# A hand-written instruction order of a convolution, norm and SwiGLU kernel is replaced: products, output steps, hidden sums and DMAs in new places

## The chip, the cores and the metric

The kernel runs on one core of one Trainium2 chip. The metric is the device time of one execution in microseconds (us); the median of the runs shown is given. The core has TensorE (PE; its weight loads, PEld, overlap its matmuls), VectorE (DVE), ScalarE (ACT), GpSimd (POOL) and SyncE (SP), which here issues nearly all DMAs. Each engine works through its own instructions in the order in which they were emitted.

## The reference

32,768 tokens of 192 values in fp32 (8 batches of 4,096 positions). First a causal convolution over the last 7 positions, its taps a softmax for each of 8 heads; then a SwiGLU feed-forward with 1,536 hidden units:

```python
w = np.exp(w - w.max(-1)); w = w / (w.sum(-1) + 1e-09)
out = np.einsum('hk,bskhg->bshg', w, x_unf)          # x_unf: 7 shifted views
...
rms = np.sqrt(np.mean(x * x, axis=-1, keepdims=True) + 1e-06)
xn = x / rms * rms_g
g = xn @ w_gate
silu = g * (1.0 / (1.0 + np.exp(-g)))
val = xn @ w_val
return (silu * val @ w_out).astype(np.float32)
```

## The kernel before

**Tiling.** The tokens go in 32 pairs of two 512-token halves (1,024 tokens). Pair 0 is computed plainly (lines 1099, 1117), pair 1 with plain gate/value products (line 890), pairs 2 to 31 in a block scheme of Strassen's kind: gate and value matrices and the two halves form 2x2 blocks, and sums of blocks are multiplied instead of blocks. Every period of the loop (w = 1 to 32) works on one pair.

**Products and steps.** A period's TensorE work is listed in `LINE`: 68 products, each with a group j = 0 to 5 (words such as P5.0, Ad.3, Q3.5), then 42 output steps (o1 to o7, each with j). A product (line 918) is six matmuls: three parts of the split operand by two halves, which write the two banks of a *bank pair*. An output step (line 945) is six smaller matmuls that multiply hidden values by blocks of the output weights. A product may open a *cell* (j and a letter a to d): P1, P5 and the A words open one. Four bank pairs exist for all cells and for the output's accumulators (`open`, `give`); a cell holds its pair until its silu and its multiply are done.

**Words of the order.** `ORDER` lists everything that is issued in one period, for all engines, in the order of emission. `pN` is the next N words of `LINE`; a minus sign behind a word means the previous pair, a plus sign the next one, two plus signs the one after. Otherwise the first letter is the engine (V VectorE, A ScalarE, G GpSimd, S SyncE) and the rest is the act:

- ga.j to gd.j: silu of a cell's gate half (line 995); ma.j to md.j: multiply with its value half (line 1002), after which the cell's pair is free.
- f1.j, f3.j: copies of finished cells (line 683; f1 opens cell b with a copy of a); f4.j, f5.j: sums that open c and d (line 989).
- h1.j to h4.j: sums of hidden values for the output steps (line 972), on VectorE or GpSimd.
- x1 to x4: sums of token blocks (line 840). n, l, d with a group 0 to 4: the three steps that split the next pair's tokens into parts (cast at line 683, differences at 826 and 828).
- cv0 to cv6: the convolution's taps (line 453; the first, on ScalarE, at 449); sq, red, pow, bc, mul: the norm (lines 464 to 503).
- pl.h: put of a normed head into DRAM (line 1062); ft.i: fetch of it, transposed, as token blocks (line 654); ld.h: load of a head of x (line 154); st: store of outputs (line 1051). The last four are DMAs in SyncE's queue.
- c1, c2, s7, C22, C21, T11 to T22: copies, sums and transposes that finish the output (lines 683, 1019, 960).

**Ring.** The split weights lie prepared in DRAM; ten slots of 192 KB hold those in use. When the last product with a slot has been issued, the next load into that slot is issued in SyncE's queue (line 798), behind whatever stands there. A load starts when its slot's last product is done, and 48 of them come in a period.

**Other orders.** `FIRST` is the order of w = 1, with W for a step of the weight preparation (lines 762 to 775) and R for the start of the ring. `PLAIN` begins the list of pair 1. The lead-in before the loop (pair 0: `conv_first`, conversion of the weights at lines 299 to 346, `START`, `LATER`) is written out by hand too. `hold` (line 226) makes a copy that the first weight loads wait for, so that x is loaded first.

Of the kernel before, what the change touches and what calls it, by code (L numbers as in the profile page):

```python
# [20 lines left out]
def kernel(  # L21
# [10 lines left out]
    nc = tc.nc  # L32
# [3 lines left out]
    H, K = weight.shape  # L36
# [21 lines left out]
    PAIRS = B * NB  # L58
# [17 lines left out]
        "a0 b0 c0 d0 o1.0 a1 b1 c1 d1 o1.1 a2 b2 c2 d2 o1.2 a3 b3 c3 d3 o1.3 a4 b4 c4 d4 o1.4",  # L76
        "a5 b5 c5 d5",
    )
    ORDER = (
# [14 lines left out]
    )  # L94
    FIRST = (
# [14 lines left out]
    )  # L110
    LINE = (
# [7 lines left out]
    )  # L119
# [10 lines left out]
    x_sb = {}  # L130
# [31 lines left out]
    def load_part(p, h, eng):  # L162

        if h == 0:
            x_sb[p] = xs.tile([P, TB + HALO, GS], F32, name="xh")
        load_head(p, p // NB, (p % NB) * PT, h, eng)
# [57 lines left out]
    def hold(t):  # L224

        nc.scalar.copy(out=t, in_=x0[:, -t.shape[1] :, 0])

# [158 lines left out]
    scr = {}  # L386

    ys = {}

    def conv_first(mine, share, give):  # L390

        t = x_sb.pop(0)
# [3 lines left out]
        for i, k in enumerate([theirs[0], mine[-1]] + theirs[1:]):  # L396
# [4 lines left out]
            if k == theirs[-1]:  # L401
                cuts = (0, H // 2, H - give)
            for lo, hi in zip(cuts, cuts[1:]):
# [4 lines left out]
                for c in range(4):  # L408
# [4 lines left out]
                    )  # L413
        for k in mine:
            xk = t[:, k : k + NJ, :]
            for h in range(share if k == mine[-1] else 0, H):
                hs = slice(h * GS, (h + 1) * GS)
                w = taps[:, h, k : k + 1]
                if k == mine[0]:
                    nc.vector.tensor_scalar(  # L420
                        out=y[:, :, hs], in0=xk[:, :, hs], scalar1=w, scalar2=None, op0=ALU.mult
                    )
                else:
                    nc.vector.scalar_tensor_tensor(
                        out=y[:, :, hs], in0=xk[:, :, hs], scalar=w, in1=y[:, :, hs],
                        op0=ALU.mult, op1=ALU.add,
                    )
# [416 lines left out]
    class Pair:  # L844
        def __init__(self, p):
            self.p = p
            self.bk, self.o_sb, self.sg = {}, {}, {}
            self.open_half, self.turned = {}, [0, 0]
            self.line = self.products()

# [75 lines left out]
        def step(self, form, k):  # L926
            b = ACC[form]
            if form in (1, 7) and b not in self.bk:
                full4.discard(self.open(b, False))
            fresh = form in (1, 7) and k == 0  # L930
            src = hs[:, k, :] if form == 5 else self.hv(k, LEFT[form])
# [126 lines left out]
    def put_away(p, h, eng):  # L1058
        if h == 0:
            scr[p] = dram.tile([D, PT], F32, name="xd")  # L1060
# [101 lines left out]
    def done(it):  # L1162
# [13 lines left out]
    LATER = (  # L1176
        (30, "s"), (35, "v"), (45, "v"), (47, "O"), (50, "O"), (53, "O"), (55, "n"), (60, "t"),
    )
# [11 lines left out]
    nc.vector.tensor_reduce(out=tp[:], in_=own[:], axis=AX.X, op=ALU.add)  # L1190
    load_in(0, nc.sync)
    load_out(0)
    load_out(1)
    load_in(1, nc.sync)
    conv_first((1, 3, 5, 6), 0, 2)
    nc.gpsimd.memset(zeros, 0.0)
# [78 lines left out]
    run([w for row in FIRST for w in row.split()], 1)  # L1275
    for w in range(2, PAIRS + 1):
        run([w for row in ORDER for w in row.split()], w)
# [28 lines left out]
```

## Time and profile before

| | us |
|---|---|
| median of 3 runs (2469.66, 2471.25, 2470.25) | 2470.25 |
| the profiled execution | 2473.39 |
| its span, first to last instruction | 2471.6 |
| start of w = 2, 3, 32 on TensorE | 214.0, 288.8, 2461.7 |
| TensorE's last matmul | 2465.9 |

The profiled execution is 3.1 us longer than the median. A period is counted from the first matmul of one pair's list to that of the next. TensorE's granted clock is 1.00 in every window. The 2,173 us from w = 3 to w = 32 are 29 periods of the same order; the 289 us before them hold pair 0, the weight preparation and pair 1. Mean lengths of one instruction, from the table of groups, in us:

| line, engine, what | us |
|---|---|
| 995 ACT silu | 0.60 |
| 1002 DVE multiply | 0.69 |
| 989 DVE f4, f5 | 1.23 |
| 972 DVE hidden sum; on POOL | 0.72 to 0.75; 1.29 to 1.73 |
| 826 DVE difference; on POOL | 1.22; 2.40 |
| 828 DVE difference | 1.25 to 1.38 |
| 840 x sum on DVE; on POOL | 0.69 to 1.25; 1.28 to 1.30 |
| 453 DVE tap | 1.81 |

### The profile page before, as it was taken

To read this page: it belongs to the slowest core of one execution; us is meant where nothing else is said; L and a number is where in the kernel's file an instruction comes from. 1 tells how busy PE (TensorE), PEld (TensorE's weight loads), DVE (VectorE), ACT (ScalarE), POOL (GpSimd) and SP (SyncE) were. 2 spreads that over 40 slices of the span, in tenths; PEclk is the share of its full clock that TensorE was granted. 3 is DMA by queue.
4 is the path that set the end of the run, shared out by engine and by line. 5 is a ranking of instruction groups with operands and counts; after the bars stand their busy time and mean duration, and the time that the engine had idled before them with its cause. 6 is when DMAs were issued, how large, how long until landed. Compare 5 with 4: busy or idle time off the path is not lost.

```text
span 2471.6 us, 69198 instructions
## 1 busy us (share of the span) xinstructions
PE 2452.5 (99%) x29136; PEld 1894.3 (77%) x29136; DVE 2024.1 (82%) x2530; ACT 1016.2 (41%) x1431; POOL 833.3 (34%) x624
## 2 busy tenths in 40 slices
PE   8999999999999999999999999999999999999999
PEld 5547778887777777877777778777787787777777
DVE  8688888889888789888888787888888888888864
ACT  6443434433344434344334344333444343443332
POOL 0541343423343323334333434233433333333322
PEclk9999999999999999999999999999999999999999
DMA  7364678666677666786667776666776666876653
GB/s 152 60 207 125 175 184 211 179 171 170 164 200 195 181 165 172 176 207 181 190 158 178 179 202 186 176 168 168 199 197 187 165 172 169 203 192 188 159 161 95
DMA packets 716392, 430.55 MB, mean 174 GB/s; under 512 B 510330, under 2 KB 702386, under 8 KB 716082
## 3 DMA queue, kind: packets, MB, share of 16 engines
q1 hardware_dynamic: 712336, 425.21, 66.5%
q8 instruction: 230, 3.77, 0.7%
q10 hardware_dynamic: 3746, 0.92, 0.2%
q14 instruction: 80, 0.66, 0.1%
HBM read 366.96 MB, written 58.98 MB: 172 GB/s over the span
## 4 chain that ended last, share of the span: by engine, by line
PE 90%; DVE 3%; DMA 3%; SPq 1%; issue 1%; POOL 1%; ACT 1%; DVEq 0%; POOLq 0%; ACTq 0%
PE ps L918 55%; PE ps L945 35%; DMA xb<-xd 1%; DMA ht<-in_moe_w_val_dram 1%; DMA ring<-wd 1%; SPq L154 0%; DVE ht L972 0%; POOL part L775 0%; SPq L238 0%; DVE ht L1117 0%; DVE ht L1002 0%; DVE part L771 0%; DVE y L453 0%; DMA x<-in_x_dram 0%; DVE ps L989 0%
## 5 line engine op out<-in xcount | busy, mean ns | idle before, releaser
L918 PE MATMUL ps<-part,ring 64*128 64x512 f32 x12240 | 1422.0, 389 | 2.6 <-DMA ring<-wd 1.9
L918 PEld LDWEIGHTS ps<-part,ring 64*128 64x128 f32 x12240 | 1152.9, 184 | 257.8 <-DVE ps L989 12.5
L995 ACT ACTIVATE tt<-ps 128x512 f32<-128x512 f32 x744 | 438.9, 599 | 715.8 <-PE ps L918 661.7
L1002 DVE TENSOR_TENSOR ht<-ps,tt 128x512 f32<-128x512 f32 x744 | 498.0, 686 | 254.3 <-ACT tt L995 252.2
L945 PE MATMUL ps<-ht,wo_sb 128*32 128x384 f32 (+2 forms) x7272 | 468.3, 380 | 0.8 <-POOL wo_sb L337 0.8
L972 POOL TENSOR_TENSOR ht<-ht 128x512 f32<-128x512 f32 x180 | 272.2, 1520 | 543.9 <-PE ps L945 536.4
L945 PE MATMUL ps<-ht,x 128*32 128x256 f32 (+2 forms) x6696 | 439.1, 379 | 1.3 <-DVE ht L972 1.3
L945 PEld LDWEIGHTS ps<-ht,wo_sb 128*32 128x32 f32 x7272 | 325.1, 110 | 114.5 <-issue 14.5
L945 PEld LDWEIGHTS ps<-ht,x 128*32 128x32 f32 x6696 | 299.6, 110 | 90.9 <-DVE ht L972 1.6
L989 DVE TENSOR_TENSOR ps<-ps,tt 128x1024 f32<-128x1024 f32 x240 | 295.8, 1233 | 54.3 <-ACT tt L683 22.8
L453 DVE SCALAR_TENSOR_TENSOR y<-xh,tp,y 128x1536 f32<-128x1536 f32 x186 | 336.6, 1810 | 0.2
L683 ACT COPY ps<-ps 128x1024 f32<-128x1024 f32 (+1 forms) x151 | 134.6, 891 | 408.0 <-PE ps L918 336.5
L972 POOL TENSOR_TENSOR hs<-ht 128x512 f32<-128x512 f32 x120 | 155.0, 1292 | 262.6 <-DVE ht L1002 262.6
L683 ACT COPY tt<-ps 128x384 f32<-128x384 f32 (+1 forms) x182 | 151.7, 833 | 218.6 <-PE ps L945 154.9
L482 POOL TENSOR_SCALAR r<-r 128x8 f32<-128x8 f32 x31 | 6.1, 197 | 504.5 <-DVE r L477 504.4
L945 PE MATMUL ps<-hs,x 128*32 128x128 f32 (+2 forms) x2232 | 161.4, 379 | 0.0
L972 DVE TENSOR_TENSOR ht<-ht 128x512 f32<-128x512 f32 x192 | 135.0, 717 | 15.2 <-PE ps L945 12.6
L945 PEld LDWEIGHTS ps<-hs,x 128*32 128x32 f32 x2232 | 106.9, 110 | 29.6
L828 DVE SCALAR_TENSOR_TENSOR part<-part,xb 128x1024 fp32r<-128x1024 f32 x87 | 120.1, 1381 | 0.0
L972 DVE TENSOR_TENSOR ht<-hs,ht 128x512 f32<-128x512 f32 x156 | 109.2, 747 | 11.3 <-PE ps L945 10.7
L826 POOL TENSOR_TENSOR part<-xb,part 128x1024 fp32r<-128x1024 f32 x29 | 69.7, 2403 | 124.0 <-PE ps L918 82.1
L503 POOL TENSOR_TENSOR xh<-y,s 128x1536 f32<-128x1536 f32 x30 | 89.9, 2995 | 15.1 <-DVE s L495 8.6
(133 smaller groups left out, 1417.6 us busy)
## 6 DMA issues: line engine op xcount, KB each, us to landing
ring<-wd SPq DMA_DIRECT2D x1440, 192.0 KB
xb<-xd SPq DMA_DIRECT2D x60, 512.0 KB
xd<-xh SPq DMA_DIRECT2D x240, 96.0 KB
xh<-in_x_dram SPq DMA_DIRECT2D x192, 105.0 KB
xb<-xd SPq DMA_DIRECT2D x60, 256.0 KB
out_dram<-o_sb SPq DMA_DIRECT2D x126, 96.0 KB
out_dram<-o_sb SPq DMA_DIRECT2D x62, 128.0 KB
wd<-part SPq DMA_DIRECT2D x5, 1152.0 KB
```

The costliest lines, as they stand in the source:

```text
L453: nc.vector.scalar_tensor_tensor(out=y, in0=xk, scalar=w, in1=y, op0=ALU.mult, op1=ALU.add)
L482: nc.gpsimd.tensor_scalar(out=r, in0=r, scalar1=s / D, scalar2=s * 1e-6, op0=ALU.mult, op1=ALU.add)
L503: e.tensor_tensor(out=yn[p].rearrange("p a t -> p t a"), in0=y, in1=ss[:].rearrange("p (t o) -> p t o", o=1).to_broadcast([P, TB, GS]), op ...
L683: nc.scalar.copy(out=dst, in_=src)
L826: e.tensor_tensor(out=split_of(g, 1).bitcast(F32R), in0=src, in1=high, op=ALU.subtract)
L828: nc.vector.scalar_tensor_tensor(out=split_of(g, 2).bitcast(F32R), in0=high, scalar=1.0 + SPLIT, in1=src, op0=ALU.mult, op1=ALU.subtract,)
L918: nc.tensor.matmul(out=self.both(j, c)[:, h, :], lhsT=left[HALF[h]], rhs=right[HALF[h]], start=(first and q == 0), stop=True, skip_group_c ...
L945: nc.tensor.matmul(out=self.acc(b)[i * Q : (i + 1) * Q, at : at + n], lhsT=left, rhs=cols, start=fresh, stop=True, skip_group_check=True, ...
L972: engine[eng].tensor_tensor(out=dst, in0=a, in1=b, op=op)
L989: nc.vector.tensor_tensor(out=self.both(j, c), in0=self.both(j, "b"), in1=s5, op=ALU.add)
L995: nc.scalar.activation(out=tt[:, t, :], in_=self.both(j, c)[:, 0, :], func=AF.Silu)
L1002: nc.vector.tensor_tensor(out=self.hv(j, "abcd".index(c)), in0=self.both(j, c)[:, 1, :], in1=tt[:, t, :], op=ALU.mult,)
```

## The change

Products, output steps and all other words of a period stand in a new order (`LINE`, `ORDER`); w = 2 has an order of its own, `SECOND`, which has the same words with stores, loads and the previous pair's end in other places. Pair 1 keeps the old sequence of output steps, now written out in `PLAIN`. Per period, two net hidden sums, x4 and l.0 go from GpSimd to VectorE; cv1 and cv2 go from the end of the period before into the period itself, among the products; d.4 goes from the beginning of a period to the end of the one before. In SyncE's queue the fetches, loads and stores stand in other places: puts and fetches in the last third of the products, loads and stores mostly among the output steps. Words that issued nothing (ft.1, ft.3) are left out. Since words can now stand in any order, three helpers no longer ask for "the first index" but for "not there yet" (`load_part`, `put_away`, `step`). In `FIRST`, ma.1 stands right behind ga.1, ahead of four steps of the weight preparation, and the loads of the pair after and the first tap (cv0) stand earlier. In the lead-in the copy of `hold` goes from ScalarE to VectorE and behind VectorE's first tap (and so do the issues of the first weight loads), one instruction of the first convolution goes from VectorE to ScalarE, and in `LATER` the conversions of the output weights (O) stand earlier.

```diff
@@ -74,48 +74,68 @@
     )
     PLAIN = (
         "a0 b0 c0 d0 o1.0 a1 b1 c1 d1 o1.1 a2 b2 c2 d2 o1.2 a3 b3 c3 d3 o1.3 a4 b4 c4 d4 o1.4",
-        "a5 b5 c5 d5",
+        "a5 b5 c5 d5 o7.0 o7.4 o1.5 o7.3 o7.1 o7.2 o2.5 o2.0 o7.5 o6.1 o6.5 o6.0 o6.4 o6.2",
+        "o6.3 o2.3 o4.0 o4.3 o5.2 o5.3 o5.1 o4.5 o5.0 o4.4 o2.2 o4.1 o2.1 o5.4 o4.2 o5.5 o2.4",
+        "o3.3 o3.1 o3.0 o3.5 o3.2 o3.4",
     )
     ORDER = (
-        "p2 Vl.2 VC22- VT11- p3- Vd.4 VT22- VT21- Vcv3+ p3- Af1.0 Af3.0 VT12- p4 Aga.0 Vcv4+",
-        "Vf4.0 Vma.0 p2 Vcv5+ p1 Sst0.4- Sst0.2- Sst1.4- Agb.1 p5 Agc.0 Aga.1 Vmb.1 Vf5.0 p3",
-        "Vcv6+ Vma.1 Vmc.0 Agb.0 Agd.0 p2 Vmb.0 Asq+ Vmd.0 p3 Af1.2 Agc.3 Af3.2 p2 Vred+ p1",
-        "Vmc.3 p1 Vf4.2 Aga.2 Vma.2 p1 Gpow+ Vbc+ p1 Vf5.2 Gmul+ p3 Spl.0+ Agd.3 Vmd.3 p3",
-        "Spl.1+ Spl.2+ Agd.2 Agb.2 Agc.2 Vmd.2 Vmb.2 Vmc.2 Spl.3+ p6 Spl.4+ Agc.1 p1 Af1.4",
-        "Spl.5+ Spl.6+ Spl.7+ Vmc.1 p3 Agd.1 Vmd.1 p2 Af3.4 p1 Vf4.4 p4 Aga.4 Sft.0+ Sft.1+",
-        "Vma.4 Vf5.4 Agb.3 p3 Agd.4 Agc.4 Vmb.3 Vmd.4 Vmc.4 p2 Sft.2+ Sft.3+ Sst0.3- Sld.0++",
-        "Sft.4+ Sft.5+ Agb.4 Sld.1++ Sld.2++ Sst1.1- Gh1.2 Vmb.4 Gh1.1 Gh3.1 Gh1.0 p1 Sld.3++",
-        "Sst0.0- Gh3.2 Sld.4++ Sst0.1- Sld.5++ Af1.5 Sld.6++ Gh1.3 Sld.7++ p1 Af3.5 p2",
-        "Sst1.0- Sst1.2- Sst1.3- Vh1.4 Vh3.4 Vh3.0 Vf4.5 An.0+ Aga.3 p3 Vma.3 p2 Gl.0+ Gh3.3",
-        "Gx3+ Vf5.5 Aga.5 Agc.5 Vma.5 Vmc.5 p3 Vx1+ Agd.5 Agb.5 An.1+ Vx2+ p11 Vmd.5 Vh2.4",
-        "Vmb.5 Vd.0+ Vh1.5 Vh3.5 Vh2.3 Vh2.1 Vh2.5 Gx4+ Gh2.0 An.4+ Ac1 p5 Vh2.2 p1 An.3+ p4",
-        "An.2+ As7 p1 Ac2 Acv0++ Vh4.0 Vd.3+ Vd.2+ p11 Vh4.5 Vl.3+ Vh4.3 Vl.4+ Vcv1++ Vl.1+",
-        "Vcv2++ Vd.1+ p3 Gh4.1 VC21 Gh4.4 Gh4.2",
+        "p1- VT11- p1- p2 Af1.0 VT21- VC22- p4- Vcv2+ p1- VT22- p1- Vl.2 p1 Vcv3+ Af3.0 VT12-",
+        "p1 Vf4.0 p2 Aga.0 p1 Vcv5+ Vma.0 p3 Vf5.0 Agc.0 p1 Agb.1 p1 Vmc.0 Vcv6+ p4 Agb.0",
+        "Vmb.1 Vcv4+ p4 Agd.0 Agc.3 Vmb.0 Vcv1+ Aga.1 p2 Vmd.0 Vma.1 Asq+ p1 Af1.2 p1 Vmc.3",
+        "Agd.3 p1 Vred+ p3 Af3.2 Aga.2 Vmd.3 Gh1.0 Vf4.2 Gh3.0 Vma.2 Gpow+ p5 Agc.2 p1 Vf5.2",
+        "Sst1.1- p2 Vbc+ Agc.1 Vmc.2 p1 Vmc.1 Agd.2 Gmul+ Agb.2 Vmd.2 p4 Af1.4 Sst0.3- Vmb.2",
+        "Agd.1 p1 Spl.5+ Spl.2+ p1 Gh1.2 p1 Spl.4+ Vmd.1 p1 Af3.4 p1 Gh1.1 Aga.4 Spl.0+ p1",
+        "Vf4.4 p1 Spl.7+ Spl.1+ Vma.4 p3 Vf5.4 Agb.3 Vh3.1 Agc.4 Spl.3+ Vmb.3 Vmc.4 p1 Spl.6+",
+        "p1 Agd.4 p2 Vmd.4 Sft.0+ Agb.4 Vmb.4 p1 Sft.2+ p1 Sld.7++ Af1.5 Sft.5+ Sld.2++ p4",
+        "Af3.5 Vf4.5 Sft.4+ p3 Aga.3 Vma.3 p1 Vf5.5 Aga.5 p2 Agd.5 Vma.5 p2 Vmd.5 Agb.5 Vh3.2",
+        "Vmb.5 p2 Vx1+ Gh1.4 An.1+ Sst1.0- Gh3.4 p1 Agc.5 Vh1.5 Vh3.5 Gh1.3 Vh2.4 An.0+ Vx2+",
+        "Vh2.0 Vmc.5 Sld.0++ p1 Sst0.2- p3 Vd.0+ Vh2.2 Gh3.3 p1 Ac1 Vd.1+ p1 Vh2.1 An.3+",
+        "Sst0.0- p3 Sld.6++ p2 Sld.3++ Vh2.3 Vh2.5 p1 Sst1.2- p2 Gx3+ Sst0.4- p1 As7 Vx4+",
+        "Vh4.3 p1 Vd.3+ Vh4.1 An.2+ p1 Vl.0+ Vl.3+ Sld.1++ p1 An.4+ Sld.4++ Vl.1+ Sst0.1- p2",
+        "Sld.5++ p1 Vh4.5 p1 Vh4.4 p1 Vl.4+ Sst1.3- Ac2 p3 Vh4.0 p1 Sst1.4- p1 Acv0++ Vd.2+",
+        "p1 Vd.4+ p1 Gh4.2 VC21",
+    )
+    SECOND = (
+        "VC22- p1 VT11- p1 p1- Af1.0 p2- VT22- VT21- p1- Vcv2+ p2- Vl.2 VT12- p1 Vcv3+ Af3.0",
+        "p1 Vf4.0 p2 Aga.0 p1 Vcv5+ Vma.0 p1 Sst0.4- p1 Sst0.2- p1 Sst1.4- Vf5.0 Agc.0 p1",
+        "Agb.1 p1 Vmc.0 Vcv6+ p4 Agb.0 Vmb.1 Vcv4+ p4 Agd.0 Agc.3 Vmb.0 Vcv1+ Aga.1 p2 Vmd.0",
...
+    )
     FIRST = (
...
-        "Vmc.0 W p1 Gpow+ W W W p1 W p1 Agd.0 W p1 Vmd.0 Vbc+ Vh1.0 p1 Gmul+ p1 Vh3.0 W",
-        "p1 Aga.1 W W W Vma.1 Vh2.0 p1 W W p1 Spl.0+ p1 Agb.1 Vmb.1 Spl.1+ p1 Spl.2+ W p1 Spl.3+ W",
+        "Vmc.0 W p1 Gpow+ W W W p1 W p1 Agd.0 W p1 Vmd.0 Vbc+ Vh1.0 p1 Gmul+ p1 Vh3.0 p1",
+        "Aga.1 Vma.1 p3 Agb.1 Vmb.1 W W W W Vh2.0 W W Spl.0+ Spl.1+ p1 Spl.2+ W p1 Spl.3+ W W",
...
-        "p9 Vh4.2 p2 Vh4.1 p2 VC21 p1 Vh4.4",
+        "Vd.0+ Vl.4+ p4 Vh4.5 p1 Vh4.0 R p1 As7 p6 Ac2 p1 Vh4.3 p9 Vh4.2 p2 Vh4.1 p2 VC21 p1",
+        "Vh4.4 Vd.4+",
     )
     LINE = (
-        "P5.0 P1.0 P2.0 Q1.0 P6.0 Ab.1 Bb.1 Eb.1 P7.0 Q2.0 Aa.1 P3.0 Ea.1 Ba.1 P4.0 Q3.0 Q4.0",
-        "P1.2 Ac.3 P5.2 Bc.3 Ec.3 P6.2 P2.2 Q1.2 Ad.3 Bd.3 P7.2 Q2.2 P3.2 Ed.3 Q3.2 Q4.2 P4.2",
-        "Ac.1 Bc.1 Ec.1 Ad.1 Bd.1 P1.4 Ed.1 P5.4 P6.4 Q1.4 Ab.3 P2.4 Bb.3 P7.4 Q2.4 P3.4 Eb.3",
-        "Q4.4 Q3.4 P4.4 P1.5 Aa.3 Ba.3 P5.5 P6.5 Ea.3 P2.5 Q1.5 P7.5 Q2.5 P3.5 Q3.5 Q4.5 P4.5",
-        "o1.0 o7.0 o1.4 o1.2 o1.3 o1.1 o7.4 o1.5 o7.3 o7.1 o7.2 o2.5 o2.0 o7.5 o6.1 o6.5 o6.0",
-        "o6.4 o6.2 o6.3 o2.3 o4.0 o4.3 o5.2 o5.3 o5.1 o4.5 o5.0 o4.4 o2.2 o4.1 o2.1 o5.4 o4.2",
-        "o5.5 o2.4 o3.3 o3.1 o3.0 o3.5 o3.2 o3.4",
+        "P1.0 P5.0 P6.0 Q1.0 Ab.1 P2.0 Q2.0 P7.0 P3.0 Bb.1 Eb.1 Q4.0 Q3.0 P4.0 Aa.1 Ea.1 Ac.3",
+        "Bc.3 Ec.3 Ba.1 Ad.3 Ed.3 P1.2 Bd.3 P5.2 P6.2 Q1.2 P2.2 Ac.1 Ec.1 P7.2 P3.2 Q2.2 Bc.1",
+        "Q3.2 Q4.2 P4.2 P1.4 Ad.1 Bd.1 Ed.1 P5.4 P6.4 Q1.4 P2.4 Ab.3 Bb.3 P7.4 P3.4 Eb.3 Q2.4",
+        "Q4.4 Q3.4 P4.4 P1.5 Aa.3 Ea.3 P5.5 P6.5 P2.5 Ba.3 Q1.5 P7.5 P3.5 Q2.5 Q4.5 Q3.5 P4.5",
+        "o1.3 o1.0 o7.1 o1.4 o1.1 o1.2 o1.5 o7.5 o7.4 o2.3 o7.2 o2.1 o2.5 o7.3 o6.0 o2.4 o7.0",
+        "o2.0 o6.3 o4.5 o4.4 o6.4 o4.0 o6.1 o4.2 o6.5 o6.2 o4.3 o4.1 o5.3 o5.2 o5.4 o5.1 o2.2",
+        "o5.5 o5.0 o3.1 o3.0 o3.5 o3.4 o3.3 o3.2",
     )
 
     cst = ctx.enter_context(tc.tile_pool(name="cst", bufs=1))
@@ -161,7 +181,7 @@
 
     def load_part(p, h, eng):
 
-        if h == 0:
+        if p not in x_sb:
             x_sb[p] = xs.tile([P, TB + HALO, GS], F32, name="xh")
         load_head(p, p // NB, (p % NB) * PT, h, eng)
 
@@ -223,7 +243,7 @@
 
     def hold(t):
 
-        nc.scalar.copy(out=t, in_=x0[:, -t.shape[1] :, 0])
+        nc.vector.tensor_copy(out=t, in_=x0[:, -t.shape[1] :, 0])
 
     def load_in(u, q):
         cols = slice(u * NF * P, (u + 1) * NF * P)
@@ -387,7 +407,7 @@
 
     ys = {}
 
-    def conv_first(mine, share, give):
+    def conv_first(mine, share, give, then):
 
         t = x_sb.pop(0)
         y = ys[0] = yp.tile([P, NJ, D], F32, name="y")
@@ -399,7 +419,7 @@
                 continue
             if k == theirs[-1]:
-                cuts = (0, H // 2, H - give)
+                cuts = (0, H // 2, H - give) if give else (0, H // 2, H // 2 + 2, H)
             for lo, hi in zip(cuts, cuts[1:]):
                 for h in range(lo, hi):
                     hs = slice(h * GS, (h + 1) * GS)
@@ -412,6 +432,8 @@
                         start=(i == 0 and lo == 0), stop=True, skip_group_check=True,
                     )
         for k in mine:
+            if k == mine[1]:
+                then()
             xk = t[:, k : k + NJ, :]
             for h in range(share if k == mine[-1] else 0, H):
                 hs = slice(h * GS, (h + 1) * GS)
@@ -846,6 +868,8 @@
             self.p = p
             self.bk, self.o_sb, self.sg = {}, {}, {}
             self.open_half, self.turned = {}, [0, 0]
+            self.begun = set()
+            self.at = {}
             self.line = self.products()
 
         def hv(self, j, c):
@@ -927,7 +951,8 @@
             b = ACC[form]
             if form in (1, 7) and b not in self.bk:
                 full4.discard(self.open(b, False))
-            fresh = form in (1, 7) and k == 0
+            fresh = (b not in self.begun) and form in (1, 7)
+            self.begun.add(b)
             src = hs[:, k, :] if form == 5 else self.hv(k, LEFT[form])
             right = RIGHT[form][:, HOME[k]]
             self.tiles(b, [right[:, m] for m in range(NM)], src, fresh)
@@ -1056,7 +1081,7 @@
         tap(p, k, eng)
 
     def put_away(p, h, eng):
-        if h == 0:
+        if p not in scr:
             scr[p] = dram.tile([D, PT], F32, name="xd")
         to = scr[p][:].rearrange("(h a) (b t) -> h b a t", a=GS, t=TB)
         queue(eng).dma_start(out=to[h], in_=yn[p][h::H])
@@ -1174,7 +1199,7 @@
         "ipvsicpsivpisvivcpsocvpispvscipvsipsiOvpsivipsvvpsopsvcpsvOnovoOpsonvOpsnoOvnopso"
     )
     LATER = (
-        (30, "s"), (35, "v"), (45, "v"), (47, "O"), (50, "O"), (53, "O"), (55, "n"), (60, "t"),
+        (30, "s"), (33, "O"), (35, "v"), (37, "O"), (44, "O"), (45, "v"), (55, "n"), (60, "t"),
     )
     heat(taps[:].rearrange("p h k -> p (h k)"), 1)
     heat(unity, 14)
@@ -1188,11 +1213,14 @@
         in1=mask[:].rearrange("p (o h) -> p o h", o=1).to_broadcast([P, K, H]), op=ALU.mult,
     )
     nc.vector.tensor_reduce(out=tp[:], in_=own[:], axis=AX.X, op=ALU.add)
-    load_in(0, nc.sync)
-    load_out(0)
-    load_out(1)
-    load_in(1, nc.sync)
-    conv_first((1, 3, 5, 6), 0, 2)
+
+    def first_loads():
+        load_in(0, nc.sync)
+        load_out(0)
+        load_out(1)
+        load_in(1, nc.sync)
+
+    conv_first((1, 3, 5, 6), 0, 1, first_loads)
     nc.gpsimd.memset(zeros, 0.0)
     nc.sync.dma_start(out=rg_sb[LOW, :], in_=rg)
     nc.sync.dma_start(out=rg_sb[UPP, 0 : KP - 1], in_=rg[:, 1:KP])
@@ -1273,7 +1301,8 @@
                     pairs[p].do(eng, name)
 
     run([w for row in FIRST for w in row.split()], 1)
-    for w in range(2, PAIRS + 1):
+    run([w for row in SECOND for w in row.split()], 2)
+    for w in range(3, PAIRS + 1):
         run([w for row in ORDER for w in row.split()], w)
 # ---- launch: one core; inputs and outputs as the reference has them ----
 _INS = ['x', 'weight', 'moe_w_gate', 'moe_w_val', 'moe_w_out', 'moe_rms_g']
```

29 rows, old and new, of tables (FIRST, SECOND) are left out of this document.

## The prediction

> **What bounds the kernel now.** I read the page's busy shares and chain first, then windows of one loop period each, then windows inside a period, then the waits of TensorE and its weight loads, and last some stretches of the timeline.
>
> ```profile
> PE 2452.5 (99%) x29136; PEld 1894.3 (77%) x29136; DVE 2024.1 (82%) x2530; ACT 1016.2 (41%) x1431; POOL 833.3 (34%) x624
> ...
> PE 90%; DVE 3%; DMA 3%; SPq 1%; issue 1%; POOL 1%; ACT 1%; DVEq 0%; POOLq 0%; ACTq 0%
> ```
>
> TensorE is the bound, and the chain that ended last runs in it for 90%. How full it is must be read from the period, not from the share:
>
> ```profile
> 744.34:819.05 74.71, 74.71 (x915) 58.65 (x914) 62.60 (x76) 30.85 (x42) 25.93 (x19) 1.00 0.72 182
> 819.05:895.03 75.98, 75.34 (x914) 58.73 (x914) 62.98 (x76) 30.94 (x42) 25.92 (x19) 1.00 0.68 179
> 895.03:970.09 75.06, 75.06 (x915) 58.54 (x914) 62.69 (x76) 30.83 (x42) 25.93 (x19) 1.00 0.69 181
> ...
> 2168.05:2242.72 74.67, 74.67 (x915) 58.62 (x914) 62.60 (x76) 30.85 (x42) 25.93 (x19) 1.00 0.71 182
> ```
>
> Columns: window, its length, busy time (and count) of PE, PEld, DVE, ACT, POOL, then clock, DMA share, GB/s. One period is one pair of token blocks. A period of 75.06 us shows PE as full as one of 74.67: short waits vanish in the modelled ends of matmuls. The Trainium skill says the same ("Perfetto Trace Analysis", section "Identifying the Most-Contended Engine": matmul busy share is a poor measure because matmuls are pipelined); by its rule the 99% leaves room for a gain, by the row alone it would leave almost none, and the periods side with the rule.
>
> ```profile
> 1580.30:1590.00 9.70, 9.70 (x88) 8.01 (x86) 1.00 0.70 222
> ...
> 1617.00:1630.00 13.00, 13.00 (x248) 9.72 (x242) 1.00 0.81 155
> ```
>
> Inside a period: gate/value products (line 918; two matmuls 0.227 us, six 0.680) and output steps (line 945; some 0.648 each). 68 x 0.680 + 42 x 0.648 + 0.84 for the four switches between the two kinds = 74.3. From the start of the loop's third period (288.78) to the last's (2461.71) there are 29 periods: 74.93 on average. So at most 0.6 per period, 18 us in all, can be won from waits; the matmuls stay.
>
> ```profile
> PEld ps L918 <- DVE ps L989: 12.5, 31, 0.5
> ...
> PEld ps L918 <- DVE ht L1002: 7.9, 30, 0.8
> PEld ps L918 <- DMA ring<-wd: 5.6, 10, 1.2
> PEld ps L918 <- ACT ps L683: 4.2, 27, 0.2
> ...
> PE ps L918 <- DMA ring<-wd: 1.9, 5, 0.8
> PE ps L890 <- DVE ht L1002: 1.4, 2, 1.2
> ...
> PE ps L945 <- DVE ht L972: 1.3, 1, 1.3
> PE ps L945 <- POOL wo_sb L337: 0.8, 1, 0.8
> ```
>
> Us in total, times, longest. Three weight-load waits come in every period; put beside TensorE's own starts they cost less than their gap: Q3.5 waits for f5.5 (line 989), it and the product ahead take 0.839 and 0.800 instead of 0.680, 0.28; P1.2 waits for the multiply that frees its bank pair (line 1002), 0.781 and 0.696, 0.12; P6.4 waits for the copy at line 683, 0.03. Mean less quiet period (74.93 - 74.70) leaves 0.23 per period, 6.7 us in 29, in a few long periods, mostly late ring loads. The last three rows are single stalls of the second pair's period and the lead-in.
>
> **The change, part by part.**
>
> *Bank pairs.* A pair is free after its last matmul's start plus 0.43 to silu, 0.60, 0.03, multiply 0.69, 0.05: 1.81. With three products between (2.04) 0.23 is left for any queue on ScalarE or VectorE. The old order has eight cells at 2.04, P1.2 among them; the new one has f1.2 and P5.5, and nearly all others at 2.72 or more, 0.91 of room. P1.2's 0.12 goes: -3.4 us over 29. P6.2 now stands two products behind P1.2 as P6.4 did behind P1.4, and Q4.5 two behind P7.5 as Q3.5 was behind its own: 0.03 and 0.28 stay. Ab.1, tightest at 1.69, is freed by a transpose (0.36 each, line 960) and not by silu and multiply.
>
> *SyncE's queue.* The old order packs token fetches, eight input loads and eight stores between 43 and 46 us of the period, among weight loads that are already urgent:
>
> ```profile
> 1538.80 2.95 SPq L1051 DMA_DIRECT2D out_dram<-o_sb  x1
> 1541.85 0.68 SPq L798 DMA_DIRECT2D ring<-wd  x1
> ...
> 1545.56 3.51 SPq L154 DMA_DIRECT2D xh<-in_x_dram  x3
> 1549.16 1.61 SPq L798 DMA_DIRECT2D ring<-wd  x3
> ```
>
> Start and length: one store holds the queue 2.95 us and three loads 3.51, and ring loads wait behind. A ring load lands 2.1 us after issue in the median and up to 6.1. The new order moves six loads and most stores into the output steps (53 to 71 us, counted by the words at 0.68 a product and 0.65 a step), where no product is due. Against it, by the same count: the puts (33 to 40) and the fetches that read them (42.1 on) are about 2 us apart at the end instead of about 7, and a fetch that waits blocks the queue. The bounds of this part are all 6.7 us won, or nothing won (or a few tenths lost per period, a rival below). I take half, -3.4: the bunch that I can point at goes, the spread of landing times doesn't.
>
> *VectorE for GpSimd.* Per period VectorE takes Vl.0 (2.40 on GpSimd, 1.22 on VectorE at line 826), x4 (1.28; 0.69) and two hidden sums (1.29; 0.69): +3.3 us; GpSimd loses 6.3. VectorE is idle some 12 of 74.7, so over the period this is covered, but the output stage is tight. Taps 1 and 2 leave it (3.5 us at their pitch of 1.73) and Vd.4 enters. By count, from P4.5's end: b's last multiply starts at +0.83, it and c's take 1.2, three x sums 2.0, 13 hidden sums at a pitch of 0.60 with dependences 8.1, nine splits at 1.13 10.2, C21 0.55: 22.9. P1.0's weights are due after 36 steps and the switch, 23.5. The room is 0.6; before it was 0.9 (C21 idled 0.89 waiting for TensorE). I allow 0.03 per period, +0.9, for the times when it runs out. In exchange, fewer GpSimd operations run beside VectorE's two-input ones. What such a meeting costs at its worst:
>
> ```profile
> 195.97 2.37 POOL L826 TENSOR_TENSOR part<-ring,part 128x1024 fp32r<-128x1024 f32 x1 [11.27 <-ACT part L683]
> 196.01 2.88 DVE L972 TENSOR_TENSOR ht<-ht 128x512 f32<-128x512 f32 x1
> ...
> 198.95 1.51 PE L945 MATMUL ps<-ht,x 128*32 128x384 f32 x24 [1.31 <-DVE ht L972]
> ```
>
> A 0.69 sum took 2.88 beside a 2.37 split on GpSimd, and TensorE waited. The Trainium skill ("SBUF — State Buffer", section "Who interferes with whom") has the rule: a VectorE instruction with two inputs in SBUF and a GpSimd instruction reading SBUF exclude each other, and the second one blocks for the whole of the first; the rows agree.
>
> *Ends, each once.* The second pair's period: Vma.1 is issued ahead of the weight preparation (line 765, 3.08 at 139.93) that held it, -1.3; the pile-up above loses its cause as output order and conv tap change, -1.5. Lead-in: the conversions of the output weights start earlier, and TensorE's 0.8 at line 945 goes. Third period: Vd.4 (1.13) stands ahead of the old pair's C22: +0.9 to +1.8, I take 1.3. End: the last turns lose the two products that ran over them, 2 x 0.33: +0.65. The small copy ahead of the first weight loads goes from ScalarE (8.94) behind VectorE's first tap (ends 9.40): +0.4 for loads first used at 23.6, hidden by 14 us; 0 here, and 0.4 if that cover is gone; I keep 0.3. Sum -1.3 - 1.5 - 0.8 + 1.3 + 0.65 + 0.3 = -1.35.
>
> *Sum:* -3.4 - 3.4 + 0.9 - 1.35 = -7.2 against the profiled execution's own 2473.4: 2466.2. That execution lies 3.1 above the median of the runs shown; I carry the distance over: **2463 us**, -0.29%. Should the 3.1 be those same irregular waits, the two overlap and the time is up to 2466.
>
> **The rivals.**
>
> R1, slower: the output stage of VectorE becomes the bound. For it: 0.6 of room after 23 us of back-to-back work, with three GpSimd operations (h3.3, x3 and h4.2, 1.3 each) still in or at the stage. Against it: most of VectorE's work there, the 19.45 busy of 20.90, ran at its pitch before. If the stage meets one GpSimd operation per period and is held 1.3, TensorE loses 1.3 - 0.55 = 0.75 per period, 22 us: 2463 - 0.9 + 22 = **2484**. It turns the sign once VectorE loses over 0.8 per output stage (0.28 x 29 = 8.1 against the other terms).
>
> R2: the irregular waits don't fall; ring loads now queue behind a fetch that waits for the puts. For it: those 2 us, and 70% DMA share in every window. Against it: after those fetches only one urgent ring load, P4.5's, is left. Without the -3.4: **2466.5**, no change to be told or just faster.
>
> R3: the change doesn't do what it says: the 0.12 only moves to another cell (f1.2 and P5.5, still at 2.04), and the ends alone count: 2470.25 - 1.35 + 0.9 = **2469.8**.
>
> **How the numbers follow.** Forecast 0.58, R2 0.18, R3 0.09, R1 0.15. A measurement of this kernel tells 0.2% (4.9 us) from no change. The forecast's own spread is 2458 to 2467, nine tenths of it under 2465.3; of R2 a third. Faster 0.58 x 0.88 + 0.06 = 0.57; same 0.07 + 0.12 + 0.08 = 0.27; slower 0.16. The range: below, all the irregular waits won (another -3.3), no loss on VectorE (-0.9), and a quarter of Q4.5's 0.28 won where f5.5 finds VectorE free sooner (-2): 2456; above, the other rivals and, of R1, somewhat over half of its 22 us: 2477. Outside lie the rest of R1 and little else.
>
> **What would show it.** Quiet periods of 74.55 to 74.60, and no row of line 918's weight loads on line 1002 with 30 times; the row on line 989 still with some 30, about 12 us; rows on ring loads at half. In the second pair's period 87 to 88.5 instead of 90.8. Wrong, if periods of 75 or more are regular, with line 945 or P1.0's weight load waiting for VectorE (lines 972, 1019): that is R1. Fetches long in SyncE's queue with ring waits after them: R2.

## The result, and the profile after

The changed kernel takes 2501.8 us (2489.7 to 2504.6, 4 runs) beside 2470.75 for the kernel before: ratio 1.0119, 95% interval 1.0104 to 1.0134, slower by 31 us. The profiled execution of the changed kernel took 2504.6 with a span of 2502.8, so against the span before (2471.6) 31.2 us have to be found.

Where they are is read from the starts of the periods, counted as before from the first product of a pair's list. (The changed order begins with two output steps of the pair before; the rows below begin there, 1.5 us ahead of that product.) The third period starts at 287.4 us instead of 288.8 (1.4 won), the 29 periods from there to the last six output steps last 76.07 on average instead of 74.93 (33.2 lost), and the rest takes 9.3 instead of 9.9 (0.6 won): 31.2. The loss is in the steady part, a little over 1.1 us per period.

The page of the changed kernel, busy shares and chain:

```profile
PE 2461.3 (98%) x29136; PEld 1948.6 (78%) x29136; DVE 2057.4 (82%) x2648; ACT 1028.4 (41%) x1431; POOL 605.1 (24%) x506
...
PE 86%; DMA 7%; SPq 3%; DVE 2%; issue 1%; ACT 0%; POOL 0%; DVEq 0%; ACTq 0%
```

GpSimd lost 228 us of work. In the chain, TensorE's share fell from 90 to 86%, and DMA with SyncE's queue (SPq) rose from 4 to 10%. Four periods of the changed kernel, columns as before:

```profile
436.61:512.68 76.07, 75.48 (x920) 59.17 (x916) 63.30 (x82) 31.30 (x42) 18.13 (x15) 1.00 0.70 179
818.80:895.46 76.66, 75.19 (x921) 59.52 (x916) 64.13 (x82) 30.66 (x42) 18.12 (x15) 1.00 0.68 175
1582.25:1658.65 76.40, 75.39 (x921) 62.41 (x916) 63.80 (x82) 32.04 (x43) 18.12 (x15) 1.00 0.70 179
2188.95:2265.07 76.12, 75.02 (x921) 64.72 (x917) 63.51 (x82) 31.50 (x43) 18.14 (x15) 1.00 0.71 178
```

The long periods are now the rule, and they show real gaps: TensorE is busy for 0.6 to 1.5 us less than the period. Waits of TensorE and its weight loads in the changed kernel (line 942 is the product, 820 the ring load, 1027 the multiply, 1044 C22 and C21):

```profile
PE ps L942 <- DMA ring<-wd: 16.4, 23, 1.4
PE ps L970 <- DVE tt L1044: 4.4, 7, 1.1
...
PEld ps L942 <- DMA ring<-wd: 24.0, 39, 1.8
...
PEld ps L942 <- DVE ht L1027: 11.0, 8, 1.5
PEld ps L970 <- DVE tt L1044: 7.8, 8, 1.6
```

Ring loads: 16.4 and 24.0 us where they had been 1.9 and 5.6. The row on line 1027 is mostly the same wait under another name: at P7.5 of one period (1631.33) the instruction waits for its ring load and for f4.5, f4.5 had ended at 1630.21, and a multiply of another cell happened to end 0.02 us before. So I set each wait beside the semaphores that the compiled instruction carries. Time lost in 29 periods by the waiting word, in us:

```
waiting word, for                  before   after    e1     e6
P7.5, ring load                      0.8     11.8    9.1    none
P4.5, ring load                      none    11.8    none   none
P2.5, Q1.5, P3.5, Q2.5, P1.5, P4.4,
  ring load                          3.8      4.4    3.8    none
Q3.5 or Q4.5, f5.5                   8.1      8.8    8.3   11.2
o3.1, P1.0, Ab.1, o7.5, VectorE      none     5.8   27.2    none
P1.2, multiply                       3.1      0.3    0.5    0.2
```

(e1 and e6 are experiments below.) Two words, P7.5 and P4.5, account for 23 of the 33 us. Some 6 us are in no row, among them 3.0 in sum at the switch behind P4.5 and 1.8 once at o7.2. The row on VectorE counts a wait against a plain product or step, so that some 5 of e1's 27.2 us are the normal switch between the two kinds: 22 are waits. What the ring loads were late by is seen in SyncE's queue, here from the middle of one period; its P7.5 was issued as the first of the three at 1627.44 and P4.5 at 1629.58:

```profile
1617.11 1.57 SPq L1076 DMA_DIRECT2D out_dram<-o_sb  x1
1618.77 0.38 SPq L820 DMA_DIRECT2D ring<-wd  x1
1619.24 1.24 SPq L1087 DMA_DIRECT2D xd<-xh  x2
1620.57 0.56 SPq L820 DMA_DIRECT2D ring<-wd  x1
1621.18 0.53 SPq L1087 DMA_DIRECT2D xd<-xh  x1
1621.81 0.56 SPq L820 DMA_DIRECT2D ring<-wd  x1
1622.42 0.53 SPq L1087 DMA_DIRECT2D xd<-xh  x1
1623.04 0.56 SPq L820 DMA_DIRECT2D ring<-wd  x1
...
1627.44 1.57 SPq L820 DMA_DIRECT2D ring<-wd  x3
1629.11 0.38 SPq L676 DMA_DIRECT2D xb<-xd  x1
1629.58 0.38 SPq L820 DMA_DIRECT2D ring<-wd  x1
```

From 1617.11 on there is no idle time in the queue. A put (line 1087) holds it for 0.53 to 0.6, and a ring load behind a put for 0.56 instead of 0.32 to 0.38. With 0.05 between issues, a put and a ring load take 1.2 us, while TensorE frees a slot nearly every product, 0.68. So with each put the queue falls further behind. Mean delay from the start of the last matmul of the product that frees a slot (it runs some 0.4) to the issue of the load into it, 26 periods, in us:

```
ring load of    P4.4   P1.5   P2.5   Q1.5   P7.5   P3.5   Q2.5   P4.5
before          3.41   3.45   0.65   0.50   0.46   0.44   0.44   0.45
after           1.02   2.37   2.88   2.19   2.88   2.85   2.68   3.02
e6              0.80   0.64   0.42   0.42   0.42   0.46   0.54   0.99
e8              3.21   3.02   3.41   2.81   2.82   2.62   2.41   2.64
e12             0.83   1.38   0.94   0.45   0.61   0.64   0.56   0.92
```

The kernel before had the same delay, but at P4.4 and P1.5, whose slots are free 7.8 us ahead of use, and it was gone by P2.5: its puts stand at 26 to 36 us of the period. In the changed kernel the norm's product ends 30.6 us behind the period's first product instead of 26.4, and cv1 and cv2, 1.81 each, had gone from the end of the period before into the products ahead of it; its puts run from 34.6 to 43.3 and meet the words whose slots are free for only 6.3 to 7.1.

From the start of its issue to the last of its sixteen semaphore updates in the trace, a load from P2.5 to Q2.5 takes 3.3 to 3.9 us on average, P4.5's 5.9, behind a fetch of 512 KB that is issued just ahead of it. In the kernel before, the loads of P7.5, P3.5 and Q2.5 took longer, 4.7 to 5.0 (3.6 to 3.9 after), and yet TensorE hardly waited, because they were issued 0.4 to 0.5 late. So the transfers became 0.9 to 1.4 us faster, which goes with the new places of the loads and stores, though no run has these alone; the delay of the issue grew by 2.2 to 2.4 and took more than that away.

### The profile page after: what moved, and what is told of

Read it like the earlier page. It is cut to its first block, busy times and chain, and to the rows that moved or that the text cites. A ratio compares the mean times of both kernels' runs of the same rounds, so it can differ in the third digit from the quotient of the medians.

```text
span 2502.8 us, 69287 instructions
## 1 busy us (share of the span) xinstructions
PE 2461.3 (98%) x29136; PEld 1948.6 (78%) x29136; DVE 2057.4 (82%) x2648; ACT 1028.4 (41%) x1431; POOL 605.1 (24%) x506
## 4 chain that ended last, share of the span: by engine, by line
PE 86%; DMA 7%; SPq 3%; DVE 2%; issue 1%; ACT 0%; POOL 0%; DVEq 0%; ACTq 0%
PE ps L942 52%; PE ps L970 30%; DMA ring<-wd 5%; PE ps L1124 2%; SPq L174 2%; PE ps L914 1%; SPq L1076 1%; DMA xb<-xd 1%; DMA out_dram<-o_sb 1%; DMA ht<-in_moe_w_val_dram 0%; DVE y L475 0%; DVE o_sb L985 0%; DMA x<-in_x_dram 0%; DVE ht L997 0%; ACT y L471 0%
## 5 line engine op out<-in xcount | busy, mean ns | idle before, releaser
L942 PE MATMUL ps<-part,ring 64*128 64x512 f32 x12240 | 1431.2, 389 | 22.1 <-DMA ring<-wd 16.4
L942 PEld LDWEIGHTS ps<-part,ring 64*128 64x128 f32 x12240 | 1206.7, 184 | 232.4 <-issue 25.1
L997 POOL TENSOR_TENSOR hs<-ht 128x512 f32<-128x512 f32 x150 | 194.1, 1294 | 900.7 <-DVE ht L1027 900.7
L970 PE MATMUL ps<-ht,x 128*32 128x256 f32 (+2 forms) x6696 | 408.9, 379 | 0.0
L970 PEld LDWEIGHTS ps<-ht,x 128*32 128x32 f32 x6696 | 285.0, 110 | 92.3 <-issue 0.8
L997 POOL TENSOR_TENSOR ht<-ht 128x512 f32<-128x512 f32 x120 | 155.6, 1297 | 717.4 <-PE ps L970 684.0
L997 DVE TENSOR_TENSOR ht<-ht 128x512 f32<-128x512 f32 x252 | 179.6, 724 | 9.5 <-PE ps L970 8.3
L970 PE MATMUL ps<-hs,x 128*32 128x128 f32 (+2 forms) x2232 | 143.2, 379 | 0.0
L997 DVE TENSOR_TENSOR ht<-hs,ht 128x512 f32<-128x512 f32 x186 | 123.4, 692 | 0.5
L848 DVE TENSOR_TENSOR part<-xb,part 128x1024 fp32r<-128x1024 f32 x87 | 105.6, 1213 | 0.0
L705 ACT CAST part<-xb 128x1024 fp32r<-128x1024 f32 x87 | 91.1, 1047 | 15.4 <-DMA xb<-xd 15.2
```

What stands on the lines that cost most here:

```text
L705: nc.scalar.copy(out=dst, in_=src)
L848: e.tensor_tensor(out=split_of(g, 1).bitcast(F32R), in0=src, in1=high, op=ALU.subtract)
L942: nc.tensor.matmul(out=self.both(j, c)[:, h, :], lhsT=left[HALF[h]], rhs=right[HALF[h]], start=(first and q == 0), stop=True, skip_group_c ...
L970: nc.tensor.matmul(out=self.acc(b)[i * Q : (i + 1) * Q, at : at + n], lhsT=left, rhs=cols, start=fresh, stop=True, skip_group_check=True, ...
L997: engine[eng].tensor_tensor(out=dst, in0=a, in1=b, op=op)
```

## The experiments

Theory A is SyncE's queue as just told. Rival B puts the loss on VectorE's output stage. All comparisons are with the kernel before.

**e1.** The fetch behind P4.5's load:

```diff
-        "p1 Agd.4 p2 Vmd.4 Sft.0+ Agb.4 Vmb.4 p1 Sft.2+ p1 Sld.7++ Af1.5 Sft.5+ Sld.2++ p4",
+        "p1 Agd.4 p2 Vmd.4 Agb.4 Vmb.4 p1 Sft.0+ Sft.2+ p1 Sld.7++ Af1.5 Sft.5+ Sld.2++ p4",
```

> The changed kernel, with one edit: the first fetch (ft.0, 512 KB) is issued one product later, behind the ring load of P4.5. Theory A (SyncE's queue: in the changed kernel ring loads are issued 2 to 3 us late behind the puts, and P4.5's load lands late behind the fetch issued just ahead of it): the waits of P4.5, 11.8 us in 29 periods, and the longer switch behind it, 2.8, mostly go; 2488 to 2494 beside 2501.8. Rival B (VectorE is late at the period's end and the ring waits only cover it): P4.5's wait goes, but the end of the output stage takes it back; within 4 us of the changed kernel.

Measured 2500.1 us (ratio 1.0118, 1.0100 to 1.0137): rival B's number. P4.5's wait is gone, 11.8 to nothing, and VectorE's waits rose from 5.8 to 27.2 (table above, switches included). Waits of weight loads and of VectorE in e1:

```profile
PEld ps L970 <- DVE tt L1044: 19.4, 24, 2.3
PEld ps L942 <- DVE o_sb L985: 9.4, 21, 0.8
PEld ps L970 <- DVE ht L997: 7.5, 12, 1.1
...
DVE tt L862 <- DMA xb<-xd: 19.4, 16, 2.0
```

VectorE waited at x1 for the fetch (19.4 us; 3.6 in the changed kernel), started its output stage late and could not catch up. So the fetch can't go back by 0.7 us, and P4.5's load can't stand in front of it, as long as both come late.

**e2.** The puts on ScalarE's queue (`Spl` to `Apl`).

> The changed kernel, with the eight puts of a period issued on ScalarE's queue in place of SyncE's, at the same places. Theory A: SyncE's queue loses eight issues of 0.55 us between 35 and 44 us of the period, so the ring loads of Q1.5 to P4.5 are issued 0.5 us after their slot is free instead of 2 to 3; ring waits fall from 47 us to 25 to 30, and the time to 2478 to 2488, if ScalarE's own chain bears eight issues of 0.6. Rival B: ring waits fall, the time stays above 2495. Rival C (the ring loads land late because the DMA engines are busy with the puts' small packets, whoever issues them): landing times stay at 4.8 us for P4.5, time above 2493.

2540.4 us (1.0285, 1.0264 to 1.0307). The part on the ring came out: delays of 0.4 to 0.8 us from P2.5 to P4.5, and no ring wait left on these words, with the same small packets in flight and P4.5's load landing 5.3 us after its issue (5.9 in the changed kernel, by the same count); so rival C falls. But ScalarE couldn't bear it. Its timeline:

```profile
1635.91 3.41 ACTq L1087 DMA_DIRECT2D xd<-xh  x3
1639.36 1.01 ACT L705 COPY tt<-ps 128x1024 f32<-128x1024 f32 x1 [2.91 <-DMA xd<-xh]
```

Three puts held ScalarE's instructions 3.4 us; f3.4 stood behind them, f4.4 behind f3.4, and TensorE waited for f4.4 at P7.4, 1.8 us a period. Its largest wait:

```profile
PE ps L942 <- DVE ps L1014: 48.9, 30, 2.9
```

**e3.** The kernel before, its eight puts at the changed kernel's places.

> The kernel before, with one edit: the eight puts stand 8 to 13 products later, at the places of the changed kernel (behind words 50 to 60 of the period), and ft.0 three words later beside ft.2. Theory A: this alone makes it slower by 15 to 30 us (2485 to 2500), with the waits on ring loads at the words behind. Rival B: the late puts alone cost under 5 us. Rival D (the new order of products leaves the ring less room): within 5 us of the kernel before.

2675.1 us (1.083, 1.0812 to 1.0848), far above all expectations, and by another way than theory A's. ScalarE's and TensorE's waits:

```profile
PE ps L918 <- DVE ps L989: 144.4, 29, 5.8
...
ACT part L683 <- DMA xb<-xd: 152.1, 29, 5.8
```

The fetch followed late puts, and in the old order the cast n.0, which needs it, stands on ScalarE ahead of ga.3; f5.5 waits for the pair that ga.3 and ma.3 free. So TensorE waited some 5 us per period. The first fetch had moved too, so this run shows how far the fetch reaches, not what the puts cost the ring.

**e4.** The lead-in's edits alone, in the kernel before.

> The kernel before, with the changes of the lead-in alone: hold's copy on VectorE behind its first tap, one more first-convolution instruction on ScalarE, conversions of the output weights earlier, and ma.1 of the second period ahead of the weight preparation. By the two traces the third period starts at 285.9 instead of 288.8; expected 1.5 to 3 us under the kernel before (2467.5 to 2469), as the pile-up at 198 us of the second period stays.

2468.4 us (0.9994, 0.9984 to 1.0003; 10 runs): 1.4 under the runs beside it, inside the interval. In its profile the third period starts at 286.9, 1.9 earlier. (The expectation's 285.9 is the start of the two output steps ahead of the changed kernel's third period, 287.4 that of its first product.)

**e5.** e1 with d.4 at the start of the next period:

```diff
-        "p1- VT11- p1- p2 Af1.0 VT21- VC22- p4- Vcv2+ p1- VT22- p1- Vl.2 p1 Vcv3+ Af3.0 VT12-",
+        "p1- VT11- p1- p2 Af1.0 VT21- VC22- Vd.4 p4- Vcv2+ p1- VT22- p1- Vl.2 p1 Vcv3+ Af3.0",
...
-        "p1 Vd.4+ p1 Gh4.2 VC21",
+        "Acv0++ Vd.2+ p2 Gh4.2 VC21",
```

> The kernel of e1 (first fetch behind P4.5's ring load), and d.4 (1.13 us on VectorE) moved from the end of the output stage to the beginning of the next period, where the kernel before had it. Theory B, VectorE's output stage is the second bound and took back what e1 won: the waits at the period's start and in the output stage (on lines 1044, 985 and 997, 27 us in e1) fall under 8, the time to 2480 to 2488. Rival A, SyncE's queue alone: within 4 us of e1's 2500.

2517.5 us (1.0191, 1.0171 to 1.0211): both expectations fell. The waits on line 1044 did fall from 16.1 to 4.9 us, but d.4 now stood ahead of the transposes that free Ab.1's pair, the tightest link at 1.69 us, and Ab.1's wait went from 4.2 to 20.3:

```profile
PEld ps L942 <- DVE o_sb L985: 30.0, 41, 1.5
```

With the fetch late, VectorE has no room on either side of the boundary; d.4's 1.1 us is paid where it stands.

**e6.** The changed kernel with its puts on GpSimd's queue:

```diff
-        return nc.scalar if eng == "A" else nc.sync
+        return nc.scalar if eng == "A" else nc.gpsimd if eng == "G" else nc.sync
...
-        "Agd.1 p1 Spl.5+ Spl.2+ p1 Gh1.2 p1 Spl.4+ Vmd.1 p1 Af3.4 p1 Gh1.1 Aga.4 Spl.0+ p1",
+        "Agd.1 p1 Gpl.5+ Gpl.2+ p1 Gh1.2 p1 Gpl.4+ Vmd.1 p1 Af3.4 p1 Gh1.1 Aga.4 Gpl.0+ p1",
```

> The changed kernel with the eight puts of a period issued on GpSimd's queue, which is idle at that time, in place of SyncE's (e2 had shown that ScalarE can't bear them). Theory A: ring loads from Q1.5 to P4.5 are issued within 1 us of their slot, their waits (28 us in 29 periods) fall under 8, time 2478 to 2485. Rival B: the ring waits fall, and waits for VectorE at the period's start rise by as much; time above 2494. Rival C (the DMA engines, not the queue): ring waits stay, time above 2494.

2470.1 us (0.9998, 0.9988 to 1.0007): the whole loss is gone, more than theory A had expected. Two periods of e6:

```profile
435.81:510.59 74.78, 74.71 (x920) 60.36 (x916) 63.49 (x82) 31.16 (x42) 22.77 (x23) 1.00 0.71 182
...
1558.15:1632.95 74.80, 74.73 (x921) 61.50 (x917) 63.49 (x82) 30.47 (x42) 22.77 (x23) 1.00 0.72 182
```

The one row that is left on ring loads, among its waits:

```profile
PEld ps L942 <- DMA ring<-wd: 0.5, 1, 0.5
```

GpSimd's and SyncE's timeline:

```profile
1590.26 1.28 POOL L1087 DMA_DIRECT2D xd<-xh  x2 [0.29 <-POOL xh L525]
...
1593.14 8.93 SPq L820 DMA_DIRECT2D ring<-wd  x9
1602.36 0.32 SPq L676 DMA_DIRECT2D xb<-xd  x1
```

The puts now start right behind the norm's product, SyncE issues ring loads as slots come free, and nearly all periods lie between 74.78 and 74.82. No wait for VectorE is left in the steady part either: with the fetch in time its output stage, 0.6 us short of TensorE's by the count, holds. That takes rival B's part as a consequence. The issuing queue is all that was changed by hand, but GpSimd also moved the puts in fewer packets (2 KB each instead of 256 bytes, by the page's table of queues); e2, with small packets, and e11 and e12 speak to that.

**e7.** e1 with x1 behind three hidden sums (`Vx1+` from ahead of `Gh1.4` to behind `Vh2.4`).

> The kernel of e1, and x1 on VectorE issued behind three hidden sums (h1.5, h3.5, h2.4) in place of ahead of them. In e1 VectorE waited 19.4 us at x1 for the fetch, and o7.5 waited 6.9 us for h3.5 behind it. Theory B: x1's wait falls under 3 us, o7.5's wait goes, and the waits at the next period's start fall by the same; 2482 to 2490. Rival A: under 4 us from e1's 2500.

2499.3 us (1.0113, 1.0098 to 1.0128). x1's wait and o7.5's are gone as expected, the rest is not: P7.5 still waits 6.7 us for its ring load, and the waits on line 1044 are 13.6 in place of 16.1 (10.9 in both without the switch): rival A's number. The order of x1 inside the stage is not what made VectorE late. ScalarE's casts of the fetched tokens, which VectorE's splits need, still waited 35.4 us for the fetch (40.8 in e1, 0.3 in e6), so the late fetch has a second way to VectorE; no run separates the two.

**e8.** Each put three words earlier.

> The changed kernel with each of the eight puts issued three words (2.0 us) earlier; the norm's product is ready at 31.8 us of the period. Theory A: the queue's lag at Q1.5 to P4.5 falls from 2.5 to 1 us or less, the ring waits there (28 us) by half or more, with nothing else touched: 2482 to 2492. Rival C: landing times rule; within 4 us of the changed kernel.

2497.6 us (1.0105, 1.0088 to 1.0122), short of theory A's expectation and, at 4.3 under the changed kernel, at the edge of rival C's. The table of delays says why: the queue now falls behind from P4.4 on (3.2 us) and is still 2.4 behind at Q2.5. Two us earlier the puts meet the same density of ring loads; P4.5's load lands 6.2 us after its issue, hardly other than the 5.9 before.

**e9, e10.** The kernel before with its puts on GpSimd's queue, and the same with e4's lead-in.

> The kernel before with its eight puts of a period on GpSimd's queue. If its long periods (6.7 us in 29) come from the same queue, they go: 2464 to 2467. If they come from the spread of landing times, 2469 to 2472.

> The kernel before with the lead-in of e4 and the puts on GpSimd's queue: 1 to 2 us under e9; 2463 to 2466, below both kernels.

2467.9 us (0.9991, 0.9982 to 1.0000) and 2465.7 (0.9983, 0.9974 to 0.9992; 10 runs of 2465.3 to 2466.9). e10 is the fastest of all, 4.1 us under the kernel before, and where it was expected; e9 lies between its two expectations. In e9's profile the mean of the 29 periods is 74.76 instead of 74.93, but e4's profile, with the puts in SyncE's queue, has 74.77. So the 6.7 us of irregular waits are mostly that one execution's, 3.1 above its median. By the medians the puts' queue is worth 2 to 3 us in the old order: 1.9 in e9, 2.7 between e4 and e10.

**e11, e12.** e6, and in SyncE's queue at the old places eight DMAs that nobody waits for: copies of the same 96 KB to a scratch place, or one row of 256 bytes each.

```diff
+    def put_extra(p, h, eng):
+        to = extra[:].rearrange("(h a) (b t) -> h b a t", a=GS, t=TB)
+        queue(eng).dma_start(out=to[h], in_=yn[p][h::H])
...
+        queue(eng).dma_start(out=extra[h:h+1, 0:TB], in_=yn[p][h:h+1, 0, :])
```

(The first `queue` line is e11's, the second stands in its place in e12.)

> The kernel of e6 (puts on GpSimd's queue, 2470) with eight DMAs of the same shape again in SyncE's queue where the puts had been, from the same tile to a scratch place that nobody reads. No fetch waits for them. Theory A (SyncE's time for eight issues is the cost): most of the 32 us come back, 2490 to 2510. Rival E (the fetches wait for the puts through SyncE's queue, and this delays VectorE): 2470 to 2476.

> As e11, but each of the eight extra DMAs moves one row of 256 bytes in place of 96 KB. If the cost is SyncE's time for an issue whatever it moves, the time lies near e11's; if it depends on the number of packets, near e6's 2470 (2470 to 2478).

e11: 2542.6 us (1.0291, 1.0273 to 1.0308). No fetch waits for these copies, and yet the loss came back, more than twice over: ring loads were issued 3.6 to 4.6 us late from P2.5 on. So rival E falls. The copies also add traffic, but from P2.5 to Q2.5 the loads landed 3.0 to 3.9 us after their issue, as in the changed kernel: the delay grew and not the transfer. That the loss is more than the changed kernel's 31 us goes with an issue of 0.68 us on average instead of 0.58 and with GpSimd's puts, which run beside it; the two weren't separated. e12: 2470.6 (1.0004, 0.9995 to 1.0013), no loss at all. SyncE's queue in e12:

```profile
1595.53 0.54 SPq L1094 DMA_DIRECT2D extra<-xh  x2
1596.16 0.34 SPq L821 DMA_DIRECT2D ring<-wd  x1
1596.55 0.27 SPq L1094 DMA_DIRECT2D extra<-xh  x1
1596.92 0.34 SPq L821 DMA_DIRECT2D ring<-wd  x1
1597.31 0.28 SPq L1094 DMA_DIRECT2D extra<-xh  x1
1597.86 0.34 SPq L821 DMA_DIRECT2D ring<-wd  x1
```

A tiny DMA and the ring load behind it take 0.27 and 0.34, 0.7 to 0.8 us with the gaps and near the 0.68 of a product, so the queue nearly keeps up. It is thus not the number of issues, but the time that each holds the queue, and this depends on what it moves.

## Why the prediction was wrong

*The bound and the periods* were read rightly: TensorE with short waits, 0.6 us per period to win at most.

*SyncE's queue, taken at -3.4, is the step that failed.* It had looked at where fetches, loads and stores go, and against it only at a fetch that waits for its puts. That wait hardly came: the fetch in the timeline above was issued in 0.38 us, and SyncE's waits of fetches for puts come to 0.9 us in the whole execution. What the prediction never priced is the time of the puts themselves, 8 times 0.58 us, in a queue with a ring load every 0.68 us. The trace before had the terms: a put's issue of 0.62 us on average, and the pace of the ring loads from the products. The term measured +36 us: 76.07 per period in the changed kernel, 74.84 in e6, times 29. Its stated bounds, from all won to a few tenths lost per period, didn't hold 1.2 lost; R2 named the right queue and gave it a loss of zero. What the term hoped for did come, transfers faster by 0.9 to 1.4 us; there the prediction had read 2.1 us for a landing in the median and 6.1 at most, where the count to the last semaphore update gives 3.3 and 7.2. Neither sign of being wrong fitted: the long periods became regular, but by ring loads behind puts, not by VectorE and not by long fetches.

*Bank pairs, -3.4:* right in kind and nearly in size; P1.2's wait fell from 3.1 to 0.3 us. Q4.5's stayed, 8.8 for 8.1, and where nothing else delays TensorE (e6) it is 11.2, 3 us more than forecast. So even there the periods are 74.8, not the 74.55 to 74.60 that were to show the forecast.

*VectorE, +0.9:* 5.8 us in the changed kernel on o3.1 and Ab.1, none in e6. That the stage fits was counted rightly; how much room it has wasn't measured, and it fits only with a fetch that is on time. R1's bound therefore stood ready behind the queue and appears in e1 (22 us), though by the late fetch and not by meeting GpSimd; it wasn't the cause here.

*The ends, -1.35:* measured -1.9, near only by luck, for the parts are others: lead-in -2.0 (forecast -0.5 with the small copy), second pair's period 90.8 to 89.0 (forecast -2.8), the next one +2.4 (+1.3), the end -0.6 (+0.65). The pile-up did lose its victim: at 196.3 us VectorE's split meets GpSimd's again and takes 3.40 instead of 1.22, as the Trainium skill's rule on shared access has it ("SBUF — State Buffer", section "Who interferes with whom"), but no matmul waits behind it.

Without the queue's part the change wins nothing: e6 stands at 2470.1 beside 2470.9, and e10, the old order with its puts on GpSimd's queue and the new lead-in, at 2465.7. Beside e10 the new order itself loses: its 29 periods are 74.84 on average instead of 74.72, and the one ahead of them is 76.96 instead of 74.69.

The Trainium skill has a sentence on the cause ("DMA: Bandwidth & Descriptors", section "Issuing engines are not separate DMA queues"): DMAs of all issuing engines run on the same 16 DMA engines, and starting them from several saves only the sequencer's time, which "is usually small relative to the DMA itself". The trace agrees that the sequencer's time is what e6 saved, with a delay of 0.4 instead of 2.9 us at P7.5. Small beside the DMA a put's 0.58 us is (3.7 from issue to landing on GpSimd's queue), but small for the kernel it was not, since other transfers queued behind it.

## What to carry to other kernels

Count a DMA queue like an engine: the issue time of everything in it, stage by stage, against the rate at which urgent transfers must be issued. Where that sum passes the stage's own pace, every later transfer is late by the difference, whatever room each had by the order. A non-urgent group of DMAs with many small packets belongs in the queue of an engine that is idle at that time, and when a stage moves, ask what its transfers will now stand among.

## What the runs showed of the hardware

The time for which SyncE's queue is held by an issue depends on the DMA: 0.27 us for one row of 256 bytes, mostly 0.32 to 0.38 for a ring load of 192 KB, 0.53 to 0.68 for 96 KB in 256-byte packets; a ring load right behind such a put mostly takes 0.56. On GpSimd's queue the same put took 0.61 of GpSimd and went out in packets of 2 KB.
